# Normalizing two tiles' softmax weights on TensorE, in a new order of the first attention layer

## The chip, the cores and the metric

The kernel runs on one core of one Trainium2 chip. The metric is the device time of one execution in microseconds; the profile is one execution recorded by the hardware profiler, and its times count from the start of its span. In the profile PE is TensorE's matmuls, PEld its weight loads, DVE is VectorE, ACT is ScalarE, POOL is GpSimd and SP is SyncE, which here only issues DMAs.

## The reference: two state-space layers and two local attentions

Four residual layers run one after the other on x of 2048 tokens by 512 features, in bfloat16:

```python
x = x + _A_ref(_layernorm(x), ...)      # a convolution as long as the sequence, from a state-space model
x = x + _B_ref(_layernorm(x), wqkv, wo) # attention
x = x + _A_ref(_layernorm(x), ...)      # the same convolution, the same weights
x = x + _B_ref(_layernorm(x), wqkv, wo)
```

The attention has 32 heads of 16 features. Every token looks at 8 keys: itself and the tokens 2, 4, ... 14 before it; keys before the first token are masked.

```python
scale = Dh ** -0.5
idx = pos[:, None] - off[None, :]             # off = 0, 2, ... 14
logits = jnp.einsum("bhsd,bhswd->bhsw", q, kg) * scale
logits = jnp.where(mask, logits, -1e9)
attn = _softmax(logits, axis=-1)              # over the 8 keys
o = jnp.einsum("bhsw,bhswd->bhsd", attn, vg)
return o.transpose(...).reshape(B, S, D) @ wo
```

## The kernel before

The program has five parts in a row: the convolution's kernel is generated (`kgen`), and then come convolution, attention, convolution, attention. All of x stays on the chip, as 16 rows j of 128 tokens by 512 features, in four groups g of four rows. The change lies in the first attention, which runs between 150 and 275 us.

**How an attention is staged** (`b_layer`). Each piece is a block of instructions with a name, and every instruction of a block is a word: the block's name and a letter.

- `y` (PE, ACT): the convolution's last matmuls for two rows and their eviction into x (L339 to L344, L1532). `n0` to `n3` is the layer norm of a group: statistics on DVE (L1158, L1161), Ln and Exp on ACT for the reciprocal deviation (L1164, L1165), then one instruction per row that applies it, on DVE (L1174) or ACT (L1172). `t` transposes the rows.
- `K`, `Q` (L1205, L1208) project to four feature tiles i of 8 heads each; `V` (L1292, L1299) projects to two tables fp of two tiles each. `M` copies rows of V between partitions with nine DMAs per table, from SP and POOL in turn (L1316), so that a token finds its keys' values in its own partition.
- `L`: logits of tile i, half jh of the sequence, and key pair w. DVE multiplies q and k (L1253, L1255), PE sums over a head's 16 features (L1277), and ACT copies the half's logits to SBUF (L1280).
- `S`: softmax of one tile and half, here called a quarter. DVE takes the maximum over keys in two steps (L1336, L1342); the 128 partitions hold the keys in two halves, so PE swaps them and DVE takes the last maximum (L1344). In tiles 0 and 1, DVE subtracts the maximum and ACT exponentiates (L1347, L1348). In tiles 2 and 3 (`pe_max`) PE subtracts it by two matmuls, identity times the logits and minus identity times the maximum, and ACT exponentiates from PSUM (L1352, L1353, L1358). PE sums over the keys (L1369). ACT takes the logarithm and then Exp of its negative, which is the reciprocal (L1378, L1379), and DVE multiplies (L1380).
- `P`: weights times V, four products of 128x2048 on DVE per tile and half (L1401), summed by PE (L1411), evicted by ACT (L1422).
- `R`: a row's output projection with x added (L1441, L1446), evicted by ACT (L1469). `N0` to `N3`: the next layer norm, with statistics on ACT where `x_sums` names the row (L1139), then the first stage of the next convolution's transform, 32 matmuls (L1486) whose evictions into Z go to ACT or DVE (L1489).

**What sets the order.** The layer's `order` is a long string of words. `Plan.run` issues the instructions in exactly this order, so each engine's queue is the string's words for that engine. Where a word can go to two engines, a trailing `+` takes the second. In this layer that is DVE and not ACT, for L1174/L1172 and for L1489. The planner also adds short matmuls of zeros where it expects TensorE to be idle (L1114).

**What exists already, unused.** `softmax` has a branch for tiles in `pe_den`; the list is empty in both layers. For them the exponentials go to a tile `e` of their own, and after the sum the branch is

```python
o = plan.add("ACT", ..., lambda: nc.scalar.activation(t.rdb[:], t.den[:], ACT.Ln, scale=DEN_SCALE), [p], drop=[p])
for k in range(n):
    p = plan.add("PE", 0.645, lambda k=k, u=u: less(k, u, True), [o], take=PA)
    got["P", i, jhs[k]] = plan.add("ACT", act_us(512), lambda k=k, u=u: exp(k, u, P, C["den_bias"][:]), [p], ...)
```

`less(k, u, True)` issues the two matmuls of L1352 and L1353 again, and as a third minus four times the identity, times the logarithm (L1355). The Exp behind it, with scale 1/4, then gives normalized weights. n is 1 here.

Of the kernel before, what the change touches and what calls it, by code (L numbers as in the profile page):

```python
# [11 lines left out]
ACT = mybir.ActivationFunctionType  # L12
ALU = mybir.AluOpType
AX = mybir.AxisListType
F32 = mybir.dt.float32
# [14 lines left out]
GE = 4  # L30
# [176 lines left out]
def z_view(Z):  # L207
    return Z[:].rearrange("k (c g) (r j e) -> k r j c g e", c=16, r=2, j=NJ)
# [652 lines left out]
class Plan:  # L861
# [44 lines left out]
    def run(self, order):  # L906
# [16 lines left out]
        if todo:  # L923
# [12 lines left out]


LAYERS = (
    dict(order="y0a y0b y0c y0d n0a n0b n0c n0e n0d n0h n0g n0i n0f y3a y3b n3a n3c y1a y1b n3b n1a n0j n0k y1c y1d n1b n0l n0p+ n0o+ n0m+ n0n "
# [27 lines left out]
         pv=[[8, 8], [8, 8], [8, 8], [8, 8]],  # L967
         soft=[0, 0, 0, 0],
         pe_max=(2, 3),
# [10 lines left out]
         third_norm=(),  # L980
         raw=[],
         y_add=[],
         pe_den=(),
         ot_any=[],
         thirds=[],
         stores=[]),
# [37 lines left out]
         third_norm=(),  # L1024
         raw=[],
         y_add=[],
         pe_den=(),
         ot_any=[],
         thirds=[12, 13, 14, 15, 10, 11],
# [18 lines left out]
def act_us(n):  # L1048
    return 0.055 + 0.00083 * n


def b_layer(nc, tc, C, Xg, Ng, Wt, last_layer, y_rows, es_y):
# [5 lines left out]
    with ExitStack() as es:  # L1058
# [5 lines left out]
        psA = pool("b_psA", 4, space=PSUM)  # L1064
# [363 lines left out]
        def out_row(j, early=False):  # L1428
# [44 lines left out]
            if last_layer:  # L1473
                got["X", j] = plan.add(dict(ACT=act_us(512), DVE=0.61), None, evict, [p], drop=[alloc])
                return
            got["X", j] = plan.add("ACT", act_us(512) + 0.095 * (j % 4 in x_sums[j // 4] and not last_layer), evict, [p], drop=[alloc])

        def dft_rows(g, normed):

            for jj in range(4):  # L1480
                for r in range(2):
                    t = SimpleNamespace()

                    def pe(jj=jj, r=r, t=t):
                        t.ps = (m.psL if r else psA).tile([128, 512], F32, name="ps_s", tag="psL" if r else "psA")
                        nc.tensor.matmul(t.ps[:], C["F1"][:, 4 * g + jj, r, :], Ng[g][:, jj, :], start=True, stop=True)  # L1486

                    def evict(eng, jj=jj, r=r, t=t):
                        (nc.scalar.copy if eng == "ACT" else nc.vector.tensor_copy)(  # L1489
                            z_view(m.Z)[:, r, 4 * g + jj], t.ps[:].rearrange("k (c e g) -> k c g e", c=16, e=GE))  # L1490
                    p = plan.add("PE", 0.22, pe, [normed[jj]], take=PL if r else PA)
                    plan.add(dict(ACT=act_us(512), DVE=0.61), None, evict, [p, x_end], drop=[p])

        def y_group(g):
            for hf in range(2):
# [40 lines left out]
        def part(name, fn, *args, **kw):  # L1536
            plan.block = name
            return fn(*args, **kw)
# [43 lines left out]
            plan.add("-", STORE_US + 0.32 * n, lambda: None, [o])  # L1582
        for j0, n in lay["stores"]:
            part(f"O{j0:x}", store, j0, n)
        with tc.manual_schedule():
            plan.run(lay["order"])
    return m.Z, es_z
# [117 lines left out]
```

## Time and profile before

| | us |
|---|---|
| three runs | 423.75, 425.57, 426.43 (median 425.57) |
| the profiled execution | 423.79 |
| its span | 422.0 |
| DVE busy in the span | 399.5 (95%) |
| PE busy | 373.6 (89%) |
| ACT busy | 329.4 (78%) |
| first attention | 150 to 275 |
| second attention | 316 to 422 |

A group's row in the profile gives the line, the engine, what is written from what, the shape and the count; then the busy time of the group in us and the mean duration of one in ns; then the idle time of the engine just before them and what ended it. Neighbours on an engine overlap, so a group's instructions are closer together than their mean duration. In a waits row stand the engine and the line that waited, the one that released it, and then the total in us, the number of waits and the longest one.

### The profile page before, as it was taken

What the parts mean: (1) busy time and instruction counts of PE and PEld (TensorE: products, weight loads), DVE (VectorE), ACT (ScalarE), POOL (GpSimd) and SP (SyncE); (2) the same over time, 40 slices, a digit from 0 to 9 for tenths busy, and PEclk for the clock granted to TensorE, in tenths of its full rate; (3) what the DMA queues carried; (4) which work ended last, traced back from release to release, by engine and by line L of the source; (5) the groups of instructions that cost most, each with busy time, mean ns of one, the idle gap of its engine ahead of it and who ended that gap; (6) DMA issues with size and microseconds to landing.
All of it is one profiled execution on the core that took longest, in us unless ns stands there. A gap on an engine that the chain in (4) does not pass through costs nothing.

```text
span 422.0 us, 12184 instructions
## 1 busy us (share of the span) xinstructions
PE 373.6 (89%) x5071; PEld 257.2 (61%) x5112; DVE 399.5 (95%) x736; ACT 329.4 (78%) x598; POOL 26.0 (6%) x68
## 2 busy tenths in 40 slices
PE   1167998999989999999997899889999999996996
PEld 1033685676458755687865565368855686875563
DVE  5999999999889989899999999999989999999994
ACT  6999999998979989757655489989988676663542
POOL 5000011011210000002010000000000001200000
PEclk9999999999999999999999999999999999999999
DMA  8900001253889950006282062239300009360022
GB/s 239 427 28 0 3 13 46 76 167 102 253 245 273 275 193 3 2 2 123 55 168 59 2 196 57 99 102 294 109 0 4 2 2 168 63 124 2 26 78 101
DMA packets 25823, 44.09 MB, mean 104 GB/s; under 512 B 7318, under 2 KB 17239, under 8 KB 25127
## 3 DMA queue, kind: packets, MB, share of 16 engines
q1 hardware_dynamic: 22918, 38.09, 31.4%
q0 software_dynamic: 1888, 4.56, 5.0%
q8 instruction: 40, 0.66, 0.7%
q10 hardware_dynamic: 960, 0.66, 0.5%
q14 instruction: 17, 0.13, 0.1%
HBM read 29.04 MB, written 6.95 MB: 85 GB/s over the span
## 4 chain that ended last, share of the span: by engine, by line
PE 39%; DVE 27%; ACT 11%; issue 6%; DMA 5%; SPq 2%; DVEq 0%; ACTq 0%
DVE prodpv L1401 11%; PE ps_qk L1205 8%; DVE prodqk L1255 5%; PE vp L291 4%; PE ps_v L1292 4%; PE psg L601 3%; PE Lp L1277 3%; ACT Z L1489 2%; DVE Z L504 2%; PE psk L568 2%; DMA Kt<-kt_scratch 2%; DMA V<-V 2%; PE ps_y L344 2%; PE pt_x L1188 2%; ACT xc L269 2%
## 5 line engine op out<-in xcount | busy, mean ns | idle before, releaser
L1401 DVE TENSOR_TENSOR prodpv<-V,Lsb 128x2048 bf16<-128x2048 bf16 x64 | 75.3, 1218 | 0.1
L1205 PE MATMUL ps_qk<-xnT,wqk 128*128 128x512 bf16 x256 | 60.1, 379 | 0.0
L1253 DVE TENSOR_TENSOR prodqk<-qT,N 128x1024 bf16<-128x1024 bf16 (+3 forms) x88 | 42.5, 538 | 2.1 <-ACT N L1208 1.8
L1255 DVE TENSOR_TENSOR prodqk<-qT,N 128x1024 bf16<-128x1024 bf16 (+3 forms) x56 | 40.5, 762 | 0.2 <-ACT qT L1208 0.2
L1411 PEld LDWEIGHTS <-prodpv 128*128 128x128 bf16 x1024 | 34.3, 98 | 9.8 <-DVE prodpv L1401 4.1
L1411 PE MATMUL po<-halves,prodpv 128*128 128x64 bf16 x1024 | 37.3, 193 | 2.9 <-DVE prodpv L1401 2.9
L275 DVE TENSOR_TENSOR pab<-xc,Kt 128x2048 bf16<-128x2048 bf16 (+1 forms) x34 | 38.6, 1151 | 0.1
L1205 PEld LDWEIGHTS <-wqk 128*128 128x128 bf16 x256 | 23.6, 98 | 23.5 <-DVE xnT L1191 0.2
L269 ACT CAST xc<-xp 128x1024 bf16<-128x1024 f32 (+1 forms) x34 | 34.7, 1035 | 2.1 <-PE xp L263 1.2
L291 PEld LDWEIGHTS <-pab 128*128 128x128 bf16 x512 | 30.4, 98 | 6.3 <-DVE pab L275 2.8
L291 PE MATMUL vp<-sb_IC,pab 128*128 128x128 bf16 x512 | 33.3, 219 | 0.9 <-ACT VT L295 0.4
L295 ACT CAST VT<-vp 128x1024 bf16<-128x1024 f32 (+1 forms) x31 | 32.5, 1079 | 0.2 <-PE vp L291 0.2
L1441 PE MATMUL ps_o<-wo_t,oT 128*128 128x512 bf16 x122 | 31.9, 379 | 0.6
L1422 ACT CAST oT<-po 128x512 bf16<-128x512 f32 x32 | 17.7, 588 | 18.5 <-PE po L1411 18.4
L1277 PEld LDWEIGHTS <-prodqk 128*128 128x128 bf16 x1024 | 29.3, 96 | 4.5 <-DVE prodqk L1255 1.8
L1277 PE MATMUL Lp<-sb_bones,prodqk 128*128 128x8 bf16 x1024 | 30.2, 166 | 1.2 <-DVE prodqk L1255 1.1
L1292 PE MATMUL ps_v<-wv,xnT 128*128 128x256 bf16 x256 | 30.3, 272 | 0.0
L528 PE MATMUL psadd<-Z,sb_ident 128*128 128x512 bf16 (+3 forms) x72 | 18.5, 339 | 12.9 <-DVE Z L504 6.9
L1299 ACT CAST V<-ps_v 128x512 bf16<-128x512 f32 x32 | 18.6, 585 | 13.2 <-PE ps_v L1292 13.1
L1158 DVE BATCH_NORM_STATS2 ln_stats<-X 128x6 f32<-128x512 bf16 x39 | 24.8, 679 | 2.8 <-ACT X L1532 2.7
L1208 ACT CAST N<-ps_qk 128x512 bf16<-128x512 f32 x32 | 18.5, 590 | 10.5 <-PE ps_qk L1205 10.2
L1292 PEld LDWEIGHTS <-xnT 128*128 128x128 bf16 x256 | 24.3, 97 | 3.6
(197 smaller groups left out, 821.7 us busy)
## 6 DMA issues: line engine op xcount, KB each, us to landing
Kt<-kt_scratch SPq DMA_DIRECT2D x60, 256.0 KB
kt_scratch<-ks SPq DMA_DIRECT2D x32, 128.0 KB
G<-c_G SPq DMA_DIRECT2D x2, 1536.0 KB
V<-V SPq DMA_DIRECT2D x8, 288.0 KB
X<-in_A_u_dram SPq DMA_DIRECT2D x4, 512.0 KB
F1Tsb<-c_F1T SPq DMA_DIRECT2D x2, 1024.0 KB
V<-V SPq DMA_DIRECT2D x4, 512.0 KB
V<-V POOLq DMA_DIRECT2D x4, 384.0 KB, 8.3
```

The lines of the kernel that those rows point to most:

```text
L269: nc.scalar.copy(xcs[cg][:, gs].rearrange("q g o l -> q (g o l)"), xps[cg][:].rearrange("q h n -> q (h n)")[:, gs.start * 128:gs.stop * 128])
L275: nc.vector.tensor_tensor(pabs[cg][:, gs], xcs[cg][:, gs].to_broadcast([128, gs.stop - gs.start, 2, 128]), kts[cg][:, gs], ALU.mult)
L291: a.last_pe = nc.tensor.matmul(vp[:, g, :], pabs[cg][:, gs.start + g, ab, :], C["IC"][:, ab, :], start=(ab == 0), stop=(ab == 1))
L295: copy(dst[..., parts(cg)[part]], vps.pop((cg, part))[:].rearrange("k g (q e) -> k q e g", e=GE))
L1205: nc.tensor.matmul(t.ps[:], wqk[:, ct, f0:f0 + 128], x_group(g)[:, :, ct], start=(ct == 0), stop=(ct == 3))
L1253: nc.vector.tensor_tensor(b.pr[:, u:u + 2 * n, 1 - halves_of[0], :], q, cols(kT[i][:, starts[0]:starts[0] + n * 128]), ALU.mult)
L1255: nc.vector.tensor_tensor(b.pr[:, u:u + 2 * n].rearrange("f u a q -> f a u q")[:, ::-1], q.unsqueeze(1).to_broadcast([128, 2, 2 * n, 64]), ...
L1277: nc.tensor.matmul(t.Lp[:, w, u % 2, u // 2, :], b.pr[:, u].rearrange("f a q -> f (a q)"), bones[:], start=False, stop=(t.parts == W // 2 ...
L1292: nc.tensor.matmul(t.ps[:, jj, :], tokens(ct, jp * 2 + jj, c), wv[:, ct, fp * 256:(fp + 1) * 256], start=(jj + ct == 0), stop=(jj == 1 and ...
L1401: nc.vector.tensor_tensor(t.p2[:, c:c + k, 0:nj, :].rearrange("p c j (d h) -> p c j d h", d=DH), m.V2[i // 2][:, c0 + c:c0 + c + k, r0:r0 ...
L1411: nc.tensor.matmul(po[jj // k][:, jj % k, c, :], t.p2[:, c - c0, jj, :], fold, start=(first and c == c0 and jj % k == 0), stop=(last and c ...
L1441: nc.tensor.matmul(t["ps"][:], m.oT[:, ft, j * 128:(j + 1) * 128], wo_t[:, ft, :], start=(start and ft == lo), stop=(ft == 3 or kept and f ...
```

## The change

In the first attention `pe_den` names the tiles 2 and 3, so that four quarters take the branch shown above in place of the reciprocal and the product on DVE (L1379, L1380). The order of the whole layer is replaced. All words of the old order are in the new one, with another engine for some of them. Three rows of layer norm pass from DVE to ACT and one eviction into Z from ACT to DVE. Ahead of the first product with V stand fewer logits products; the first such product is of tile 1 and not of tile 0; tile 2's first products with V1 come ahead of P18.

Around it the planner gets four additions that issue nothing in this layer. `z_split` is empty in both layers. The eviction of x in rows without sums may now go to DVE, but no word of the order asks for it. Five words at the end (`Ca` to `Ce`) stand for the first steps of the next convolution and have no instruction behind them. The eviction into Z has bounds for its columns, which keep their full width. The second attention keeps its order and its lists.

```diff
 LAYERS = (
-    dict(order="y0a y0b y0c y0d n0a n0b n0c n0e n0d n0h n0g n0i n0f y3a y3b n3a n3c y1a y1b n3b n1a n0j n0k y1c y1d n1b n0l n0p+ n0o+ n0m+ n0n "
...
-               "L211a V110a V102b S11f V110b V113a V113b V112a V103a V103b V112b V100a S11g S11h V100b L200c L212a L201c L211b L212b S01j P00a "
...
-               "L301b P18a L303c S20i S20j L300c L302c S21c L301c P10l L303d P18b P18c Q32a Q32b P18i S30a S21d P18g S30b P18d P18j S21e P18e "
...
-               "S30h S30i P18l P18k P20i P20a P20g P20b P20c S30j P20e P20j P20d P20h P20f P20l R7a P30e P30a P20k P30b P30c P30f P30g P30d P30h "
...
+    dict(order="y0a y0b y0c y0d n0a n0c n0b n0d n0e n0i n0g y1a y1b n1a n0h n1b n0f n1c y1c y1d n1d n0j n0k n0l y2a y2b n1e n1i n1g n1f n1h n0p "
...
+               "V102b V112a V112b V113b V110a V100a V101a V100b V110b V101b V103a V103b P10g S01e M1a M1y M1g M1m P10i P10a S01f P10e P10b "
...
+               "P00d L213d S20f S20g S20h L300c S20i S20j L301c L302c S01j L303c P20a S21a L303d S30a P00j P00f S21b S30b P20g Q32a P00l P00k "
...
+               "Ca Cb Cc Cd Ce",
          pv=[[8, 8], [8, 8], [8, 8], [8, 8]],
...
-         pe_den=(),
+         z_split=[],
+         pe_den=(2, 3),
...
-            got["X", j] = plan.add("ACT", act_us(512) + 0.095 * (j % 4 in x_sums[j // 4] and not last_layer), evict, [p], drop=[alloc])
+            if j % 4 in x_sums[j // 4]:
+                got["X", j] = plan.add("ACT", act_us(512) + 0.095, evict, [p], drop=[alloc])
+                return
+            got["X", j] = plan.add(dict(ACT=act_us(512), DVE=0.61), None, evict, [p], drop=[alloc])
+
+        firsts, seconds = [], []
...
-                    def evict(eng, jj=jj, r=r, t=t):
+                    def evict(eng, c0=0, c1=16, jj=jj, r=r, t=t):
...
+                    split = [4 * g + jj, r] in lay["z_split"]
+                    pool = PA if not r else PO if split else PL
...
+        if not last_layer:
+            plan.block = "C"
+            p = plan.add("PE", 0.44, lambda: None, firsts, take=PA, cols=0)
+            plan.add("-", 0.0, lambda: None, [p], drop=[p])
+            o = plan.add("DVE", 0.6, lambda: None, [p] + seconds)
+            p = plan.add("PE", 0.43, lambda: None, [o], cols=0)
+            plan.add("ACT", 0.905, lambda: None, [p] + seconds)
```

More of the change, by code (lines that the diff above doesn't have):

```diff
@@ L1026 @@
          y_add=[],
+         z_split=[],
          pe_den=(),
@@ L1484, in pe @@
                     def pe(jj=jj, r=r, t=t):
-                        t.ps = (m.psL if r else psA).tile([128, 512], F32, name="ps_s", tag="psL" if r else "psA")
+                        t.ps = dict(psA=psA, psL=m.psL, psO=m.psO)[t.pool].tile([128, 512], F32, name="ps_s", tag=t.pool)
                         nc.tensor.matmul(t.ps[:], C["F1"][:, 4 * g + jj, r, :], Ng[g][:, jj, :], start=True, stop=True)
-                    def evict(eng, jj=jj, r=r, t=t):
+                    def evict(eng, c0=0, c1=16, jj=jj, r=r, t=t):
                         (nc.scalar.copy if eng == "ACT" else nc.vector.tensor_copy)(
-                            z_view(m.Z)[:, r, 4 * g + jj], t.ps[:].rearrange("k (c e g) -> k c g e", c=16, e=GE))
-                    p = plan.add("PE", 0.22, pe, [normed[jj]], take=PL if r else PA)
-                    plan.add(dict(ACT=act_us(512), DVE=0.61), None, evict, [p, x_end], drop=[p])
+                            z_view(m.Z)[:, r, 4 * g + jj, c0:c1], t.ps[:, c0 * 32:c1 * 32].rearrange("k (c e g) -> k c g e", c=c1 - c0, e=GE))
+                    split = [4 * g + jj, r] in lay["z_split"]
+                    pool = PA if not r else PO if split else PL
+                    t.pool = pool[0]
+                    p = plan.add("PE", 0.22, pe, [normed[jj]], take=pool)
+                    if not split:
+                        firsts.append(plan.add(dict(ACT=act_us(512), DVE=0.61), None, evict, [p, x_end], drop=[p]))
+                        continue
+                    us = dict(ACT=act_us(256), DVE=0.34)
+                    halves_of = [plan.add(us, None, lambda eng, c0=c0, evict=evict: evict(eng, c0, c0 + 8), [p, x_end]) for c0 in (0, 8)]
+                    firsts.append(halves_of[0])
+                    seconds.append(halves_of[1])
+                    plan.add("-", 0.0, lambda: None, halves_of, drop=[p])
         def y_group(g):
```

49 rows, old and new, of the table LAYERS are left out of this document.

## The prediction

> **What bounds the kernel now.** I read the busy times of the page first, then the busy time by stretches of the first attention (it runs from 150 to 275.3 us), then VectorE's waits in it, and last the groups of instructions by form and the timeline.
>
> ```profile
> PE 373.6 (89%) x5071; PEld 257.2 (61%) x5112; DVE 399.5 (95%) x736; ACT 329.4 (78%) x598; POOL 26.0 (6%) x68
> ```
>
> The stretches are rows of start:end, length, and then the busy time of PE, PEld, DVE, ACT and POOL with their instructions, the clock (1.00 in all of them) and the DMA share:
>
> ```profile
> 150.00:175.00 25.00, 24.89 (x185) 14.01 (x185) 22.96 (x64) 21.51 (x35) 0.00 (x0) 1.00 0.15 49
> 175.00:205.00 30.00, 30.00 (x454) 22.56 (x453) 29.05 (x67) 19.13 (x38) 2.25 (x4) 1.00 0.30 63
> 205.00:245.00 40.00, 35.33 (x627) 25.81 (x629) 40.00 (x56) 22.11 (x50) 2.19 (x4) 1.00 0.29 61
> 245.00:275.30 30.30, 27.76 (x331) 15.26 (x334) 29.54 (x59) 29.53 (x76) 0.00 (x0) 1.00 0.39 123
> 150.00:275.30 125.30, 117.98 (x1588) 77.64 (x1595) 121.55 (x243) 92.28 (x198) 4.44 (x8) 1.00 0.29 74
> ...
> 170.00:180.00 10.00, 10.00 (x112) 6.46 (x111) 8.68 (x20) 6.90 (x12) 0.00 (x0) 1.00 0.01 2
> 220.00:230.00 10.00, 8.56 (x199) 6.71 (x199) 10.00 (x17) 5.26 (x12) 0.00 (x0) 1.00 0.38 91
> 230.00:240.00 10.00, 7.24 (x146) 5.32 (x145) 10.00 (x11) 3.61 (x9) 0.00 (x0) 1.00 0.02 3
> ```
>
> VectorE is the first bound: 121.55 of 125.30 us, and 40.00 of 40.00 between 205 and 245. TensorE is a near second up to 220 (30.00 of 30.00 from 175 to 205) and has 4.2 us free between 220 and 240 (1.44 + 2.76). ScalarE has much room until 245 and none after: 29.53 of 30.30, as much as VectorE there. The last stretch thus has two bounds, the one before it one and a half. What VectorE waits for:
>
> ```profile
> DVE ln_stats L1158 <- ACT X L1532: 1.4, 1, 1.4
> DVE prodqk L1253 <- ACT N L1208: 0.9, 1, 0.9
> DVE ln_nb L1166 <- ACT ln_rstd L1165: 0.6, 1, 0.6
> ```
>
> These 2.9 us could at best be won by order alone; everything else must come from work taken off VectorE. The second attention (from 316 us on) and both convolutions keep their order and their code, so a difference at 275 is carried to the end.
>
> **The change part by part.** The prices are these groups of the first attention, and four pieces of the timeline and the chain that show how far neighbours overlap:
>
> ```profile
> L1174 DVE TENSOR_SCALAR N<-X,ln_rstd,ln_nb 128x512 bf16<-128x512 bf16 x30 | 10.9, 404 | 0.1
> L1253 DVE TENSOR_TENSOR prodqk<-qT,N 128x1024 bf16<-128x1024 bf16 x20 | 13.3, 684 | 1.2 <-ACT N L1208 0.9 <-ACT qT L1208 0.3
> L1489 DVE CAST Z<-ps_s 128x512 bf16<-128x512 f32 x10 | 6.4, 678 | 0.0
> L1336 DVE TENSOR_TENSOR sm_m<-Lsb 128x256 bf16<-128x256 bf16 x8 | 2.3, 284 | 0.0
> L1344 DVE TENSOR_TENSOR sm_mx<-sm_m,ps_max 128x128 bf16<-128x128 bf16 x8 | 2.2, 279 | 0.0
> L1342 DVE TENSOR_TENSOR sm_m<-sm_m 128x128 bf16<-128x128 bf16 x8 | 1.7, 217 | 0.0
> L1380 DVE TENSOR_TENSOR Lsb<-Lsb,sm_rdb 128x512 bf16<-128x512 bf16 x8 | 3.3, 417 | 0.0
> ...
> L1489 ACT CAST Z<-ps_s 128x512 bf16<-128x512 f32 x22 | 11.7, 611 | 0.0
> L1358 ACT ACTIVATE Lsb<-ps_sub 128x512 bf16<-128x512 f32 x4 | 2.4, 599 | 2.5 <-PE ps_sub L1353 2.5
> L1379 ACT ACTIVATE sm_rdb<-den 128x128 bf16<-128x128 f32 x8 | 2.2, 279 | 0.2
> L1172 ACT ACTIVATE N<-X,ln_nb,ln_rstd 128x512 bf16<-128x512 bf16 x2 | 1.6, 812 | 0.0
> ...
> 166.88 3.45 PE ps_qk L1205 x16
> 254.92 4.62 DVE L1401 TENSOR_TENSOR prodpv<-V,Lsb 128x2048 bf16<-128x2048 bf16 x4
> 270.72 4.50 ACT L1489 CAST Z<-ps_s 128x512 bf16<-128x512 f32 x9
> 272.58 2.54 DVE L1489 CAST Z<-ps_s 128x512 bf16<-128x512 f32 x4
> ```
>
> Four evictions on VectorE fill 2.54 us, so the next starts 0.62 after one that lasts 0.678; neighbours on VectorE overlap by some 0.06 to 0.08. On ScalarE nine fill 4.50: 0.49 apart at 0.611, an overlap of 0.12. A matmul of 512 columns costs TensorE 3.45 / 16 = 0.216.
>
> *Off VectorE: the product with the reciprocal sums.* `pe_den=(2, 3)` takes one such product (L1380) out of each of four quarters (feature tiles 2 and 3, two halves each): 4 x (0.417 - 0.08) = 1.35 us.
>
> *Onto TensorE.* Each of the four gets three matmuls of 128x512 (the logits again, minus the maximum, minus four times the logarithm): 12 x 0.216 = 2.6 us. They fall where tiles 2 and 3 are normalized, in the old trace from about 218 us on; TensorE has 4.2 us free in 220 to 240, so I cost them at nothing. Without that cover they cost 2.6.
>
> *Onto ScalarE.* An Exp of 128x512 (0.599 - 0.12 = 0.48) replaces an Exp of 128x128 (0.279 - 0.11 = 0.17): 4 x 0.31 = 1.2 us. Three quarters lie before 245, where ScalarE has 18 us free in 40; one (tile 3, second half) lies near 250.
>
> *Against it speaks a rule.* The Trainium skill, page "ScalarE: Activation LUTs", section "Rules for kernel authors", says to do multiplications on VectorE and not on ScalarE. It counts the instruction and not the queue: by it each quarter loses 0.31 on ScalarE and 0.65 on TensorE for 0.34 won, and where ScalarE set the pace the time would rise. The busy rows say that this can be so only after 245; the second rival is that case.
>
> *The new order: who does what.* Counting the words of both orders, all instructions stay, but three rows of normalization (L1174 to L1172) pass from VectorE to ScalarE, and one eviction of the transform (L1489) passes back: VectorE -3 x 0.33 + 0.62 = -0.37, ScalarE +3 x 0.69 - 0.49 = +1.6. Two of the three rows belong to the first group of the second normalization (N0) and so to ScalarE's full last stretch. In all VectorE gets 1.35 + 0.37 = 1.7 us less, ScalarE 2.8 more, TensorE 2.6 more.
>
> *The new order: first half.* Group 1 of the first normalization now comes ahead of group 3, and the first product with V is of tile 1, not tile 0. Ahead of that product the new order issues less on both engines: two logits blocks and a sum on TensorE, and on VectorE two logits products of 1024 (0.6 each), a subtraction (0.34, the size of L1380) and a normalized row (0.33), 1.9 us in all, which come behind it instead. VectorE's waits in this half (1.4, 0.9 and 0.6) may go or be doubled: -2.9 to +2.9, and I take 0.
>
> *The new order: the copies of V.* V1's rows are copied between partitions by SP and POOL; POOL has nothing else, and behind V1's copies on SP come only the loads of the next convolution's kernel spectrum (L230).
>
> ```profile
> 192.62 3.83 SPq L1316 DMA_DIRECT2D V<-V  x3
> ...
> 197.58 7.81 DMA V<-V
> ...
> 210.47 2.19 SPq L1316 DMA_DIRECT2D V<-V  x3
> 211.78 6.12 SPq L1316 DMA_DIRECT2D V<-V  x3
> 210.74 2.19 POOL L1316 DMA_DIRECT2D V<-V  x4 [15.60 <-ACT V L1299]
> 207.23 4.62 DVE L1401 TENSOR_TENSOR prodpv<-V,Lsb 128x2048 bf16<-128x2048 bf16 x4
> 229.09 3.49 DVE L1401 TENSOR_TENSOR prodpv<-V,Lsb 128x2048 bf16<-128x2048 bf16 x3
> ```
>
> V0's copies were issued from 192.62 and landed at 205.39 (197.58 + 7.81): 12.8 us. The first product with V started at 207.23; in the new order it is due 1.9 earlier, at 205.3, and V0's last eviction stands behind the same amount of TensorE's work as before: a wait of 0.1. V1's copies, issued from 210.47, land by the same 12.8 at 223.2. The first product with V1 is at 229.09 now. In the new order the four products of P18, six small steps of the maxima of tiles 2 and 3, a product with reciprocals and a normalized row come behind it: 4 x 1.135 + 1.07 (twice 0.20, 0.14 and 0.20) + 0.34 + 0.33 = 6.3 us, so it is due at 222.8. Both margins (1.8 and 5.9 us) are gone: together 0 (each read needs only some of the copies) to 0.4 by these rows, and I take 0.4. Behind a waiting product stands all of VectorE's queue.
>
> *The last stretch.* From the end of the last product with V (254.92 + 4.62 = 259.54) to the last eviction (272.58 + 2.54 = 275.12) pass 15.6 us. In the new order one eviction more on each of VectorE and ScalarE comes behind that point, but 1.7 + 0.6 = 2.3 us of VectorE's work less ahead of it. So the point comes 2.3 us earlier and the rest is at least 0.6 longer, which is the same 1.7. ScalarE's rest is longer by 0.49.
>
> **The sum.** -1.7 (VectorE) + 0 (TensorE, ScalarE, first half) + 0.4 (copies of V) = -1.3 us. The profiled execution took 423.79 us, 1.8 more than its span of 422.0, so it would be 422.5. The median of the three runs shown is 425.57, 1.8 above the profiled one; on the scale of medians the forecast is 424.3 us, 0.3% below. About 1% (4.3 us) is what a measurement of this kernel can tell from no change.
>
> **Rivals.**
>
> *VectorE starves for TensorE; slower than before.* Place: 170 to 250 us, where TensorE's queue is in order and nearly full. For: TensorE waits in that queue for ScalarE when it sums the exponentials, and the new subtraction adds the same kind of wait for the logarithm:
>
> ```profile
> 227.99 0.38 PE L1369 MATMUL den<-Lsb,halves 128*128 128x128 bf16 x4 [0.69 <-ACT Lsb L1358]
> ```
>
> If each of the four quarters holds TensorE for two such waits, 4 x 2 x 0.65 = 5.2, then with 2.6 of work 7.8 us meet 4.2 free: 3.6 late, less 1.7 won, +1.9: 427.5 as a median. It decides from 1.7 us of lateness on; the order puts logits or V work of TensorE between most of these steps, which speaks against it. If also the first half fits as badly as in 170 to 180, where VectorE stood for 1.32 of 10 us, in each of the five stretches of 10 us up to 220 and not in one, that is 4 x 1.32 = 5.3 more, 433 at the worst.
>
> *ScalarE sets the last stretch; no change.* It gets 2 rows (1.4), one longer Exp (0.31) and an eviction less (-0.49) in the stretch that is full at 29.53 of 30.30: +1.2, while the stretch starts 1.3 earlier by what VectorE saved ahead of it. Sum 0: 425.5. Against it: the new order also starts ScalarE's work of this stretch earlier.
>
> *V1's copies come later than 223.2.* If the last one, whose issue ends at 217.9 (211.78 + 6.12), needs from there the 7.8 us that V0's last took from its issue, it lands at 225.7: a wait of 2.9 us instead of 0.4, and the time is 426.8, 1.2 above before. It decides from a landing at 224.5 on.
>
> *Order wins too.* VectorE's 2.9 us of waits shrink to none and V1 is in time: -1.7 - 2.9 = -4.6 us, 421.0. Against it: the first 1.4 is the start behind the first rows, which both orders share.
>
> **How the numbers follow.** Forecast 0.45; starving TensorE 0.22; ScalarE 0.12; V1's copies 0.07; order wins 0.14. The likeliest alone gives 424.3 with 422.5 to 426 (first half and copies of V). For 8 in 10 the range reaches to 420.5 on the side of the winning order, and to 429.5 into the starving case, whose far end stays out. Faster by over 1% is most of the winning order and a little of the forecast's spread: 0.16. Slower by over 1% is the worse part of the starving case: 0.17. The rest, 0.67, is within 1%.
>
> **What would show it.** Right: L1380 falls from 16 to 12, a Ln that writes bf16 and 12 more matmuls of 512 columns; VectorE still at 10 of 10 from 205 to 245, its busy time in the first attention near 119.9; the next convolution's first transposes some 1.3 us earlier. The copies' term shows as a wait of the first product with V1 on a DMA. The starving rival shows as waits of `prodqk` or the maxima on TensorE, with TensorE's new waits on the logarithm above 0.5 us each. ScalarE as the bound shows as VectorE idle after 245 with ScalarE at 10 of 10. The forecast is wrong if the attention ends later than 275 or before 272, or if the second attention's length differs by more than 0.5 us.

## The result and the profile after

The kernel after takes 423.84 us, the median of 11 runs (422.63 to 426.24), beside 425.61 us for the kernel before, the median of 11. The ratio is 0.9959 with a 95% interval of 0.9939 to 0.9979: 1.7 us faster (0.9 to 2.6). The forecast was 424.3.

The profiled execution of after does not show this by its total: it took 424.25 us, and that of before 423.79. VectorE's timeline says why. First before, at the first statistics of the attention, the first transposes of the next convolution, and the first statistics of the second attention (start, duration, then the instruction):

```profile
153.65 2.58 DVE L1158 BATCH_NORM_STATS2 ln_stats<-X 128x6 f32<-128x512 bf16 x4 [1.37 <-ACT X L1532]
...
275.94 0.69 DVE L254 COPY zt<-pt 128x1024 bf16<-128x1024 bf16 x1 [0.81 <-PE pt L248]
...
308.88 2.58 DVE L1158 BATCH_NORM_STATS2 ln_stats<-X 128x6 f32<-128x512 bf16 x4 [1.34 <-ACT X L1532]
```

And the same places of after:

```profile
154.73 2.58 DVE L1160 BATCH_NORM_STATS2 ln_stats<-X 128x6 f32<-128x512 bf16 x4 [1.37 <-ACT X L1549]
...
276.06 0.69 DVE L254 COPY zt<-pt 128x1024 bf16<-128x1024 bf16 x1 [0.80 <-PE pt L248]
...
309.01 2.58 DVE L1160 BATCH_NORM_STATS2 ln_stats<-X 128x6 f32<-128x512 bf16 x4 [1.35 <-ACT X L1549]
```

The attention starts 1.08 us later in this execution, behind code that is the same in both kernels; over all the profiles of this study that start lies between 153.65 and 155.23. It then gives back nearly all of the delay. So the attention is measured here from its first statistics to its last eviction into Z. This last row is ScalarE's, before:

```profile
270.72 4.50 ACT L1489 CAST Z<-ps_s 128x512 bf16<-128x512 f32 x9
```

and after:

```profile
270.88 4.47 ACT L1496 CAST Z<-ps_s 128x512 bf16<-128x512 f32 x9
```

The length is 275.22 - 153.65 = 121.57 before and 275.35 - 154.73 = 120.62 after; two more profiles of after gave 120.07 and 120.64 (mean of the three 120.44). Within just these bounds, the busy times of PE, PEld, DVE, ACT and POOL, before:

```profile
153.65:275.22 121.57, 114.36 (x1550) 75.22 (x1555) 119.30 (x238) 89.19 (x194) 4.44 (x8) 1.00 0.27 67
```

and after, with the stretches that the prediction showed of before:

```profile
154.73:275.35 120.62, 116.59 (x1566) 75.88 (x1563) 117.89 (x232) 92.07 (x196) 4.48 (x8) 1.00 0.28 68
...
150.00:175.00 25.00, 24.91 (x192) 14.30 (x193) 22.44 (x63) 21.80 (x35) 0.00 (x0) 1.00 0.20 67
175.00:205.00 30.00, 30.00 (x449) 22.08 (x448) 28.98 (x68) 19.10 (x39) 2.25 (x4) 1.00 0.33 63
205.00:245.00 40.00, 38.23 (x675) 27.64 (x673) 39.51 (x53) 24.68 (x54) 2.23 (x4) 1.00 0.24 48
245.00:275.30 30.30, 28.09 (x310) 15.02 (x306) 29.95 (x58) 30.09 (x75) 0.00 (x0) 1.00 0.46 141
```

VectorE has 1.41 us less to do and is idle for 2.73 instead of 2.27. TensorE has 2.2 more; between 205 and 245 its free time shrinks by 2.9, from 4.67 (40 - 35.33) to 1.77. ScalarE has 2.9 more. The groups by form show the new pieces:

```profile
L1357 PE MATMUL ps_sub<-sm_rdb,sb_nident 128*128 128x512 bf16 x4 | 1.5, 378 | 0.0
L1360 ACT ACTIVATE Lsb<-ps_sub,den_bias 128x512 bf16<-128x512 f32 x4 | 2.8, 697 | 1.5 <-PE ps_sub L1357 1.5
L1360 ACT ACTIVATE sm_e<-ps_sub 128x512 bf16<-128x512 f32 x4 | 2.4, 602 | 0.9 <-PE ps_sub L1355 0.9
L1374 ACT ACTIVATE sm_rdb<-den 128x128 bf16<-128x128 f32 x4 | 1.1, 278 | 1.2 <-PE den L1371 1.1
L1382 DVE TENSOR_TENSOR Lsb<-Lsb,sm_rdb 128x512 bf16<-128x512 bf16 x4 | 1.7, 422 | 0.0
L1176 DVE TENSOR_SCALAR N<-X,ln_rstd,ln_nb 128x512 bf16<-128x512 bf16 x27 | 9.7, 410 | 0.1
L1496 DVE CAST Z<-ps_s 128x512 bf16<-128x512 f32 x11 | 7.2, 686 | 0.3 <-PE ps_s L1493 0.3
```

The products with the reciprocals (L1380 before, L1382 now) fall from 8 to 4 in this attention, the rows on VectorE from 30 to 27, its evictions into Z rise from 10 to 11. VectorE's waits:

```profile
DVE ln_stats L1160 <- ACT X L1549: 1.4, 1, 1.4
DVE prodqk L1255 <- ACT N L1210: 1.0, 3, 0.6
...
DVE prodpv L1403 <- DMA V<-V: 0.4, 1, 0.4
```

The wait for the first rows stays, the one for `ln_rstd` is gone, and one for the copies of V is new.

### The profile page after: what moved, and what is told of

Same layout as the page of the kernel before. It is cut to its first block, busy times and chain, and to the rows that moved or that the text cites. A ratio compares the mean times of both kernels' runs of the same rounds, so it can differ in the third digit from the quotient of the medians.

```text
span 422.4 us, 12235 instructions
## 1 busy us (share of the span) xinstructions
PE 379.3 (90%) x5120; PEld 259.1 (61%) x5120; DVE 398.4 (94%) x730; ACT 332.7 (79%) x600; POOL 26.0 (6%) x68
## 4 chain that ended last, share of the span: by engine, by line
PE 46%; DVE 25%; ACT 7%; DMA 6%; issue 4%; SPq 2%; DVEq 0%; ACTq 0%
PE ps_qk L1207 10%; DVE prodpv L1403 9%; PE ps_v L1294 5%; DVE prodqk L1257 4%; PE vp L291 3%; PE psg L601 3%; PE Lp L1279 3%; PE po L1413 3%; PE ps_o L1443 2%; DVE Z L504 2%; DVE pab L275 2%; DMA Kt<-kt_scratch 2%; PE psk L568 2%; DMA V<-V 2%; ACT Z L1496 2%
## 5 line engine op out<-in xcount | busy, mean ns | idle before, releaser
L1413 PEld LDWEIGHTS <-prodpv 128*128 128x128 bf16 x1024 | 35.3, 100 | 7.2 <-DVE prodpv L1403 2.0
L1443 PE MATMUL ps_o<-wo_t,oT 128*128 128x512 bf16 x128 | 33.0, 379 | 0.0
L528 PE MATMUL psadd<-Z,sb_ident 128*128 128x384 bf16 (+3 forms) x75 | 18.7, 337 | 13.1 <-DVE Z L504 7.9
```

Source lines behind the costliest of these rows:

```text
L1413: nc.tensor.matmul(po[jj // k][:, jj % k, c, :], t.p2[:, c - c0, jj, :], fold, start=(first and c == c0 and jj % k == 0), stop=(last and c ...
L1443: nc.tensor.matmul(t["ps"][:], m.oT[:, ft, j * 128:(j + 1) * 128], wo_t[:, ft, :], start=(start and ft == lo), stop=(ft == 3 or kept and f ...
```

## The experiments

All ratios are to the kernel before on the same chip. Lengths, busy and idle times are of VectorE from the attention's first statistics to its last eviction into Z, in one profile each.

| run | ratio (95%) | median us | length | busy | idle |
|---|---|---|---|---|---|
| before, four groups | 1 | 425.61, 425.29, 424.94, 425.48 | 121.57 | 119.30 | 2.27 |
| after | 0.9959 (0.9939 to 0.9979) | 423.84 | 120.62 | 117.89 | 2.73 |
| after_again | 0.9958 (0.9939 to 0.9977) | 423.69 | 120.07 | 117.78 | 2.29 |
| after_third | 0.9967 (0.9945 to 0.9989) | 424.43 | 120.64 | 117.86 | 2.78 |
| order_only | 0.9988 (0.9961 to 1.0014) | 425.72 | 122.05 | 119.37 | 2.68 |
| order_only_2 | 0.9997 (0.9972 to 1.0021) | 425.96 | 122.79 | 119.45 | 3.34 |
| den_old_order | 1.0031 (1.0009 to 1.0053) | 426.69 | 123.46 | 118.33 | 5.13 |
| den_old_moved | 1.0023 (1.0000 to 1.0046) | 425.84 | 121.42 | 118.14 | 3.28 |
| rows_back | 1.0001 (0.9984 to 1.0019) | 424.60 | 121.89 | 118.33 | 3.56 |
| dve_more | 1.0114 (1.0084 to 1.0145) | 429.92 | 126.80 | 123.68 | 3.12 |
| pe_more | 1.0141 (1.0117 to 1.0166) | 430.98 | 126.28 | 118.51 | 7.77 |
| act_more | 1.0003 (0.9987 to 1.0020) | 424.88 | 121.45 | 117.97 | 3.48 |
| v_later | 0.9953 (0.9931 to 0.9976) | 423.52 | 120.06 | 117.77 | 2.29 |
| den_both | 1.0017 (0.9994 to 1.0041) | 426.58 | 120.37 | 117.86 | 2.51 |

One profile's length and the ratio, which stands on 5 to 12 runs, agree to within 1.4 us. Where they differ the text says so.

In the windows of two of these profiles TensorE's granted clock (the number ahead of the last two in a row) was not 1.00 throughout: it was 0.58 between 224 and 228 in order_only_2, and 0.83 between 225 and 235 in dve_more. Just there VectorE waited for TensorE, 0.85 and 0.39 us, which the first attention of no other profile of this order shows; the two lengths are too long by about that much. In order_only_2:

```profile
224.00:228.00 4.00, 3.32 (x54) 2.59 (x53) 3.69 (x8) 1.50 (x3) 0.00 (x0) 0.58 0.03 9
...
228.58 0.29 DVE L1346 TENSOR_TENSOR sm_mx<-sm_m,ps_max 128x128 bf16<-128x128 bf16 x1 [0.85 <-PE ps_max L1342]
```

### The change again

The same kernel as after, in the first group of runs and once more in the last.

> The changed kernel once more, beside the three that follow. Expected 0.996 of before, -1.7 us, as measured; the profile's first attention should again be about 1 us shorter from its first statistics to its last eviction (121.5 us before, 120.5 after).

> The changed kernel a third time, as the mark for the three others on the same chip: ratio 0.996, first attention 120.1 to 120.6 us from its first statistics to its last eviction.

Measured: 0.9958 and 0.9967. With the first 0.9959 the effect stands in three groups of runs, between -1.4 and -1.8 us.

### The order alone

```diff
-         pe_den=(2, 3),
+         pe_den=(),
```

> The new order with the normalization as before, on VectorE. Theory A: three rows less and an eviction more on VectorE (-0.37 us), the wait for V0's copies of 0.45 us still there, so about 0, ratio 0.999 to 1.001. Theory B: the whole gain is here, -1.7 us, ratio 0.996.

> The new order without the normalization on TensorE, a second time, to tell 0 from a small loss: its first attention was 0.5 us longer than before's in one profile (122.05 against 121.57 us), its ratio 0.9988 with 0.9961 to 1.0014. If the order is worth nothing by itself: 0.998 to 1.002, and 121.6 to 122.2 us for the first attention.

Measured: 0.9988 and 0.9997, no difference by either interval. The window of its attention:

```profile
154.99:277.04 122.05, 114.53 (x1558) 74.89 (x1556) 119.37 (x236) 90.85 (x196) 4.47 (x8) 1.00 0.28 67
```

VectorE's busy time is that of before, 119.37, though three rows went to ScalarE for one eviction. Against after, which differs only in the normalization, VectorE has 1.5 us more to do (119.37 and 119.45 to 117.84, the mean of three) and the attention is 1.6 and 2.3 us longer than the mean of 120.44. Without the 0.85 us at the lower clock the second is 1.5 us longer, and its length, which missed the expected 121.6 to 122.2, lies inside. By the ratios the step is 0.0030, 1.3 us, in each of the two groups in which both kernels ran (0.9958 beside 0.9988, 0.9967 beside 0.9997). So in the new order the normalization is worth what it takes off VectorE, and TensorE's extra work costs nothing that can be seen.

### The normalization alone, in the old order

The kernel before with its list filled. One word, S21j, had to move behind P18h: it is now the Exp that frees a buffer in PSUM, and S30i takes that buffer before S21j's old place.

```diff
-         pe_den=(),
+         pe_den=(2, 3),
...
-  ... S30c S30d P18h S30e ...   ... L311a S21j L311b ...
+  ... S30c S30d P18h S21j S30e ...   ... L311a L311b ...
```

> The old order with the normalization of tiles 2 and 3 on TensorE alone (one word, S21j, moves forward, because its new instruction frees a PSUM buffer that S30i takes). Theory A (VectorE sets the pace until 245): four products of 0.34 us less on VectorE and nothing else, -1.35 us, ratio 0.997. Theory B (the order brings the gain, and the normalization costs what it adds to ScalarE and TensorE): 0 to +1.2 us, ratio 1.000 to 1.003.

Measured: 1.0031, slower by 1.3 us; the interval excludes the gain of theory A. Theory B has the size nearly right, but its reason, that the normalization costs what it adds, does not hold in the new order. VectorE did get less to do, and waited for more:

```profile
155.23:278.69 123.46, 117.24 (x1566) 76.17 (x1564) 118.33 (x234) 90.90 (x194) 4.44 (x8) 1.00 0.28 66
```

Its timeline has three waits that neither before nor after has:

```profile
227.98 0.29 DVE L1336 TENSOR_TENSOR sm_m<-Lsb 128x256 bf16<-128x256 bf16 x1 [0.56 <-ACT Lsb L1280]
...
231.47 0.29 DVE L1344 TENSOR_TENSOR sm_mx<-sm_m,ps_max 128x128 bf16<-128x128 bf16 x1 [0.60 <-PE ps_max L1340]
...
258.63 4.63 DVE L1401 TENSOR_TENSOR prodpv<-V,Lsb 128x2048 bf16<-128x2048 bf16 x4 [1.86 <-ACT Lsb L1358]
```

The third comes from a place in a queue. The last matmul of the subtraction on TensorE, and ScalarE's timeline:

```profile
256.54 0.38 PE L1355 MATMUL ps_sub<-sm_rdb,sb_nident 128*128 128x512 bf16 x1
...
257.43 0.58 ACT L1422 CAST oT<-po 128x512 bf16<-128x512 f32 x1 [0.87 <-PE po L1411]
257.91 0.69 ACT L1358 ACTIVATE Lsb<-ps_sub,den_bias 128x512 bf16<-128x512 f32 x1
```

The subtraction of S31 ends at 256.92, but its Exp stands behind an eviction that itself waits for TensorE, and VectorE's product with these weights waits 1.86. The Trainium skill, page "PSUM — Partial Sum Buffer", section "Engine vs sequencer instructions", calls the queues of ScalarE and VectorE strictly first in, first out; the Exp at 257.91 behind the waiting eviction agrees. The second wait is of the same kind on TensorE: the subtraction of S21 stands ahead of the swap for S30's maximum.

The first wait is of another kind. S30's first maximum needs logits that ScalarE evicts at 227.36 (L303d), two places behind the new Exp of S20. TensorE and ScalarE there:

```profile
225.24 0.18 PE L1277 MATMUL Lp<-sb_bones,prodqk 128*128 128x8 bf16 x1 [0.64 <-issue]
225.70 0.38 PE L1355 MATMUL ps_sub<-sm_rdb,sb_nident 128*128 128x512 bf16 x1
226.78 0.54 PE L1277 MATMUL Lp<-sb_bones,prodqk 128*128 128x8 bf16 x16
...
226.12 0.69 ACT L1358 ACTIVATE Lsb<-ps_sub,den_bias 128x512 bf16<-128x512 f32 x1 [1.38 <-PE ps_sub L1355]
226.71 0.58 ACT L1422 CAST oT<-po 128x512 bf16<-128x512 f32 x1
227.36 0.58 ACT L1280 CAST Lsb<-Lp 128x512 bf16<-128x512 f32 x1
```

TensorE's sums for these logits end at 227.32, and the eviction starts 0.04 us later, when ScalarE was through with what stood ahead of it (226.71 + 0.58 = 227.29): TensorE held it, not the Exp's place. TensorE was late by the three matmuls of the subtraction (0.65 us) and by 0.64 us of idle time for which the trace names no cause ("issue") and which neither before nor after shows.

### The normalization in the old order, four words moved

The words at these three places are moved.

```diff
- P18a L303c S20i S20j L300c L302c S21c L301c P10l L303d P18b
+ P18a L303c S20i L300c L302c S21c L301c P10l L303d S20j P18b
...
- S21g S21h S21i S30c S30d P18h
+ S21g S21h S30c S21i S30d P18h S21j
...
- S31h S31i N0v N1b P28h P28l N0j+ S31j
+ S31h S31i N0v S31j N1b P28h P28l N0j+
```

> The old order with the normalization on TensorE, and now four of its words moved in their queues: the new Exp S20j behind the eviction of the logits L303d, the new subtraction S21i behind the maximum's swap S30c, S21j forward, and the new Exp S31j ahead of two evictions that wait for TensorE. In the run without these moves VectorE waited 0.56, 0.60 and 1.86 us at S30a, S30d and P38a, 3.0 in all. Theory A' (what was lost is the place of the new instructions in queues that are served in order): the waits go, the first attention shrinks from 123.5 to about 120.6 us, ratio 0.997. Rival (the old order leaves no room for them at all, the whole new order is needed): at least 122.5 us, ratio 1.000 or more.

Measured: the attention is 2.0 us shorter than in den_old_order, 121.42, and the two waits near 230 are gone; the third is halved:

```profile
256.19 4.63 DVE L1401 TENSOR_TENSOR prodpv<-V,Lsb 128x2048 bf16<-128x2048 bf16 x4 [0.90 <-ACT Lsb L1358]
```

Two of the three moves did this. The second wait (0.60) went with S21i behind the swap, and the third fell by 0.96 with S31j ahead of the eviction: 1.56 of the 2.0 us. The first went with TensorE's idle time of 0.64 us and not with S20j, since here too the eviction of the logits starts when TensorE has them:

```profile
226.54 0.58 ACT L1280 CAST Lsb<-Lp 128x512 bf16<-128x512 f32 x1 [1.33 <-PE Lp L1277]
```

That two of the waits came from the words' places is so shown, in one profile each. That the time falls with them is not: by the ratios the two kernels lie 0.3 us apart, with about 0.9 us to either side of each, and den_old_order's profile was one of its slower runs (427.62 us, median 426.69). The expected ratio of 0.997 was missed: it is 1.0023. Of the 0.9 us that this median lies above before, the length (0.15 shorter than before) gives nothing; this profile's attention also starts late, at 155.20, and whether that is more than scatter stays open.

### More work on each engine

Three kernels after, each with extra work in tiles 2 and 3: sixteen products of 128x512 on VectorE, four behind each last maximum;

```diff
+                    for _ in range(4):
...
+                        nc.vector.tensor_tensor(junk[:], P(), over_keys(t.mx[:]), ALU.mult)
```

> The changed kernel with four more products of 128x512 on VectorE in each quarter of tiles 2 and 3, written to a tile that nothing reads: 16 x 0.34 = 5.4 us. Theory A: they come out one to one against the changed kernel, +5.4 us, ratio to before 1.0085. If ScalarE or TensorE set the pace by now, the cost is below 2 us, ratio 1.000 or less.

thirty-two matmuls of 128x512 on TensorE, eight with each subtraction of the logarithm;

```diff
+                for _ in range(8 if by_den and not last_layer else 0):
+                    nc.tensor.matmul(u.ps[:], ident[:], P()[:, k], start=True, stop=True)
```

> The changed kernel with eight more matmuls of 128x512 ahead of each new subtraction, into the same PSUM bank, which the real ones then start anew: 32 x 0.216 = 6.9 us of TensorE. In the changed kernel TensorE has 1.8 us free in the 40 us from 205 on. If the 2.6 us of the change were covered by that room and the room is now used up: +4 to +5 us, ratio 1.006 to 1.008. If TensorE has room elsewhere too: below +2, ratio 1.000 or less.

and twelve copies of 128x512 on ScalarE, four behind each new Exp but the last, which lies in the last stretch.

```diff
+                        for _ in range(4 if (i, a) != (3, 1) and not last_layer else 0):
...
+                            nc.scalar.activation(junk[:], t.e[:, k], ACT.Identity)
```

> The changed kernel with four more copies of 128x512 on ScalarE behind the new Exp of three quarters (both of tile 2, the first of tile 3), to a tile that nothing reads: 12 x 0.48 = 5.8 us ahead of the last stretch, where ScalarE has 15 us free in 40. Theory A: hidden but for queueing, below +1 us, ratio 0.996 to 0.998. If ScalarE's additions are on the path: +3 to +6 us, ratio 1.003 to 1.010.

Measured against the mean of after (120.44 us; 117.84 busy on VectorE, 92.03 on ScalarE): VectorE's busy time rises by 5.8 and the length by 6.4, of which 0.39 is the wait at the lower clock, so 1.0 per us. TensorE gets 32 x 0.216 = 6.9 and the length rises by 5.8, so 0.85 per us. ScalarE's busy time rises by 5.3 (97.33) and the length by 1.0, so 0.2 per us. By the ratios, with 0.9961 as the mean of after, the three cost 6.5, 7.7 and 1.8 us, so 1.1, 1.1 and 0.3 per us; pe_more's profile, at 428.83 us, is the fastest of its five runs (median 430.98). So VectorE and TensorE cost about the same, and ScalarE a third of it or less. By the ratios each cost more than expected (5.4, 4 to 5, and below 1 us). TensorE's price is the surprise. VectorE's longest wait in pe_more:

```profile
DVE prodpv L1405 <- ACT Lsb L1362: 3.3, 3, 1.5
```

and TensorE in the stretch of tiles 2 and 3:

```profile
205.00:245.00 40.00, 38.60 (x590) 26.26 (x588) 36.82 (x50) 20.93 (x44) 2.22 (x4) 1.00 0.24 48
```

The change's 2.6 us on TensorE fitted in the free time; 6.9 more don't, and come back as products that wait for the Exp behind the late subtraction. Two causes are not separated here: the used-up room (1.4 us of 40 are still free), and the place of the added matmuls, eight (1.7 us) ahead of each Exp. ScalarE's additions stand behind the Exp, where they delay less; no run has the additions at other places. In act_more VectorE's new wait is small:

```profile
DVE sm_m L1338 <- ACT Lsb L1282: 1.1, 2, 0.7
```

### The rows back on VectorE

The three rows return to VectorE and the eviction to ScalarE, at the same places of the order.

```diff
- ... n1m ... N0l ... N0j ... N0p+ ...
+ ... n1m+ ... N0l+ ... N0j+ ... N0p ...
```

> The changed kernel with engines as in the old order for three rows of layer norm (n1m, N0j, N0l back to VectorE) and one eviction into Z (N0p back to ScalarE); all places stay. VectorE gets 3 x 0.33 - 0.62 = 0.37 us more, ScalarE 1.6 less. Theory A (VectorE sets the pace, the passing of rows is worth 0.37): +0.4 us, ratio 0.997. If ScalarE sets the last stretch: 1 us faster than the changed kernel, ratio 0.993.

Measured: 1.0001, 1.7 us slower than after, and a length of 121.89, 1.45 longer; the prediction priced this term at 0.37.

```profile
153.90:275.79 121.89, 116.88 (x1565) 75.88 (x1563) 118.33 (x234) 90.50 (x194) 4.47 (x8) 1.00 0.28 67
```

VectorE's busy time rises by 0.5 as costed; the rest is idle time. Its timeline in the last stretch:

```profile
262.01 0.69 DVE L1160 BATCH_NORM_STATS2 ln_stats<-X 128x6 f32<-128x512 bf16 x1 [0.47 <-ACT X L1471]
263.48 1.88 DVE L1160 BATCH_NORM_STATS2 ln_stats<-X 128x6 f32<-128x512 bf16 x3 [0.77 <-ACT X L1471]
```

Statistics wait 1.24 us for evictions of X on ScalarE, which after does not show. ScalarE's timeline there, and its row of X in after:

```profile
259.87 1.07 ACT L1424 CAST oT<-po 128x512 bf16<-128x512 f32 x2 [0.61 <-PE po L1413]
261.39 0.60 ACT L1471 ACTIVATE X<-ps_o 128x512 bf16<-128x512 f32 x1 [0.45 <-PE ps_o L1443]
261.88 0.58 ACT L1496 CAST Z<-ps_s 128x512 bf16<-128x512 f32 x1
262.34 1.60 ACT L1471 ACTIVATE X<-ps_o 128x512 bf16<-128x512 f32 x3
```

```profile
261.30 2.06 ACT L1471 ACTIVATE X<-ps_o 128x512 bf16<-128x512 f32 x4
```

ScalarE is not full here: it waits for TensorE, 0.61 and 0.45 us, and TensorE's sums follow VectorE's last product with V, which ends 0.6 later than in after (259.13 - 153.90 = 105.23 from the first statistics, beside 104.64). Then the eviction into Z that went back to ScalarE stands between those of X. So in the last stretch a swap of work between two engines isn't priced by VectorE's busy time alone: its delay comes back to it through TensorE and ScalarE, and what ScalarE does first there, VectorE waits for.

### A logits product ahead of the first product with V

The word L211b, a logits product of 128x512 on VectorE (0.34 us from start to start, not the 0.87 of the expectation), is moved ahead of P10g, the first product with V, so that V0's copies get that much longer.

```diff
- V103a V103b P10g S01e ... Q31a L211b L212a
+ V103a V103b L211b P10g S01e ... Q31a L212a
```

> The changed kernel with one logits product of tile 2 (L211b, 0.87 us) moved ahead of the first product with V on VectorE; nothing else. In profiles of the changed order that product waited 0.45, 0.00, 0.24, 0.35 and 0.42 us for V0's copies. If this wait is a term of the time: the wait is gone, -0.3 us against the changed kernel, ratio to before 0.995. If it only moves (the next steps that need L211b are behind the same TensorE work): no difference, 0.996.

The first product with V in after, after_third and v_later, one row each:

```profile
207.37 1.23 DVE L1403 TENSOR_TENSOR prodpv<-V,Lsb 128x2048 bf16<-128x2048 bf16 x1 [0.45 <-DMA V<-V]
```

```profile
207.29 1.23 DVE L1403 TENSOR_TENSOR prodpv<-V,Lsb 128x2048 bf16<-128x2048 bf16 x1 [0.49 <-DMA V<-V]
```

```profile
206.16 1.22 DVE L1403 TENSOR_TENSOR prodpv<-V,Lsb 128x2048 bf16<-128x2048 bf16 x1
```

The wait is gone and the attention is as short as the shortest of after, which also had no such wait. The ratio, 0.9953, is the lowest of the study, but its interval covers after's three: a version that is at least as good, not one shown to be better.

### The same in the second attention

```diff
-         pe_den=(),
+         pe_den=(2, 3),
```

in the second layer's list, with seven words (S20i, S20j, S30i, S30j, S21j, S31i, S31j) moved by hand to places where TensorE and ScalarE have other work between the logarithm and the subtraction.

> The changed kernel with tiles 2 and 3 of the second attention normalized on TensorE as well; seven words of that layer's order (S20i, S20j, S30i, S30j, S21j, S31i, S31j) stand where TensorE and ScalarE have other work between the logarithm and the subtraction. If VectorE sets the pace there as in the first attention and the places are good: -1.35 us more, ratio to before 0.993. If the queues lose it again, as in the old order of the first attention: 0 to +1.5 us against the changed kernel, ratio 0.996 to 1.000.

Measured: 1.0017, 2.4 us slower than after (0.9961) and worse than either expectation. The first attention is as before this edit (120.37); the second has new waits of VectorE:

```profile
DVE prodpv L1403 <- ACT Lsb L1360: 3.2, 3, 1.6
...
DVE sm_mx L1346 <- PE ps_max L1342: 0.7, 2, 0.5
```

They are 3.9 us where four products of 1.4 us in all were saved. As in den_old_order, VectorE waits for new Exps and for maxima whose inputs come late, in an order that wasn't made for the new instructions.

## Why the prediction was right, point by point

**The forecast.** 424.3 was said and 423.84 measured; the ratio forecast, 0.997, lies within 0.9939 to 0.9979. The parts hold too, taken by ratio: the order alone was summed at 0.0 (-0.37 for the rows, +0.4 for the copies) and measured -0.1 and -0.5 us; the normalization on top of it was summed at -1.35 and is (0.9961 - 0.9993) x 425.4 = -1.4. That the order came out at nothing is in part luck: it holds two errors of about 1 us, told below, that cancel (the second is inferred).

**What bounds the kernel.** VectorE, as read: 1.0 to 1.1 us per us added. TensorE as a near second with 4.2 us free is right as well: the change's 2.6 went in without a trace in VectorE's idle time (2.3 to 2.8, beside 2.7 and 3.3 with the order alone), and further work costs 0.85 to 1.1, no less than on VectorE. ScalarE's room until 245 is real: 0.2 to 0.3.

**The rule of the Trainium skill** (page "ScalarE: Activation LUTs", section "Rules for kernel authors": multiplications on VectorE) did not decide here. ScalarE took the longer Exp at 0.2 to 0.3 per us and VectorE gave up the products at 1.0 to 1.1.

**The products, -1.35.** Measured -1.5 in busy time (after against order_only).

**The rows, -0.37.** Mis-sized. In busy time they are -0.5 (rows_back), but their worth is 1.45 us in length and 1.7 by ratio. The step that failed is the count of VectorE's work alone in the last stretch, which the prediction itself had called a stretch of two bounds; rows_back shows the waits of 1.24 us that it leaves out.

**The first half, 0.** This is where the rows' larger worth seems to go: the order alone gives no gain that the interval shows, though it contains the rows. If the worths add up, the order with neither the rows nor the normalization would cost 1.4 us (0.0 in rows_back, less the -1.4); no run has that. VectorE's busy time with the order alone is 119.37 and not 119.30 - 0.5 = 118.8, so 0.6 us is lost in small amounts over many instructions; no single wait carries it, and its cause was not settled. This error and the one in the rows, of opposite sign, largely cancel in the measured ratios.

**The copies of V, +0.4.** The size is right, 0.45 in after and 0.49 in after_third (none in after_again), the place is not, so the term came out by luck: the wait is V0's, put at 0.1, and not V1's. The first product with V1 didn't wait:

```profile
224.83 1.23 DVE L1403 TENSOR_TENSOR prodpv<-V,Lsb 128x2048 bf16<-128x2048 bf16 x1
```

**The last stretch.** The last product with V was to end 2.3 us earlier and the rest to take 0.6 longer. From the first statistics it ends 1.2 to 1.8 earlier (104.64, 104.11, 104.67 beside 105.89), and the rest takes 0.3 longer.

**The rivals.** Starving for TensorE did not come: the subtraction of the logarithm (L1357) has 0.0 us of idle time before it. In den_old_order the time did rise, by 1.3 us, near the +1.9 of the rival, but not by its waits: TensorE has 0.0 us of idle time before the subtraction of the logarithm there too (L1355), where the rival put 0.65. What came late was work behind the new matmuls in TensorE's queue, and an Exp behind an eviction in ScalarE's. The place of the words decides, as the sentence on the order against this rival had it. ScalarE as the bound did not come: in after, VectorE stays busy for 29.95 of the last 30.30 us, and rows_back, which takes 1.5 us off ScalarE, is slower. V1's copies were in time. The order did not win alone.

**The tests.** Two of them were badly put. "The attention ends later than 275" happened (275.35), and the next convolution's transposes came 0.12 later and not 1.3 earlier, because this execution reached the attention 1.08 us late; counted from the first statistics they come 1.0 earlier. A busy time of 119.9 from 150 to 275.3 fails likewise, since that window then holds other work. VectorE was busy for 39.51 of 40 us from 205 to 245 and not for all 40: the wait for V0's copies lies there. Bounds must be tied to an event of the stage and not to the clock of one execution. The second attention's start stood as said: 33.66 us behind the last eviction in both kernels, and from there to the end of the span pass 113.4 us beside 113.1, within the 0.5 that was allowed.

## What to carry to other kernels

Taking work off the engine that bounds a stage pays only where the replacement's instructions fit into the in-order queues of the other engines: the same edit gave -1.4 us in an order made for it and +1.3 us in the old one. The traces show VectorE waiting where a new instruction stands ahead of work that is ready, or behind work that is not; moving two such words took 1.56 us of these waits away in the trace, but won no time that the runs show. Price a shift of work by what each engine costs per microsecond in that stage (here about 1 on VectorE, about as much on TensorE once its free time is used up, 0.2 to 0.3 on ScalarE), not by which engine is quicker at the operation, and follow a delay through the engines that come next until it returns. For gains below 1%, compare the length of the stage between two of its own events, since the start of a stage can move by as much, and look at the granted clock inside it.

## What the runs showed of the hardware that was not expected

- The Exp that takes its bias from a tile lasts 697 ns where the same form without it lasts 602 (the two rows of L1360): 95 ns more. The Trainium skill, page "ScalarE: Activation LUTs", section "What ACT_TABLE_LOAD costs", gives 93 ns for a pointer operand of one value per partition; the rows agree. The prediction took 599 for it, 0.4 us too little on ScalarE over four.
- The first statistics of the attention come between 153.65 and 155.23 us in fourteen profiles whose code up to there is the same: 1.6 us, as much as the effect itself.
- TensorE's granted clock falls for a few us in single executions: it was 0.50 from 225 to 228 in order_only_2, and VectorE waited 0.85 us at its end. Of the 93 runs of the kernel before that stand beside the experiments, the 34 with a mean granted clock of 0.998 or more took 424.5 us on average and the other 59 took 426.0.
